# V projected like K and Q, then block-transposed on VectorE, in a fused attention and token-mixing kernel on one core

## The chip, the cores and the metric

The kernel runs on one core of one Trainium2 chip. The metric is the device time of one execution in microseconds, from start to end, as the median of several runs. A core has five engines with a queue each: TensorE (PE in the profile; its weight loads are PEld), VectorE (DVE), ScalarE (ACT), GpSimd (POOL), and SyncE (SP), which here only issues DMA transfers. Each engine works through its own queue strictly in order and meets the others only at semaphores.

## The reference

The program runs two layers, each an attention block followed by a token-mixing block, on x of 2048 tokens and 512 features. Both blocks normalise x and are added to it.

```python
def _A_ref(x, wqkv, wo):
    B, S, D = x.shape
    H = 32; Dh = D // H; W = 256
    qkv = (x @ wqkv).reshape(B, S, 3, H, Dh).transpose(2, 0, 3, 1, 4)
    q, k, v = qkv[0], qkv[1], qkv[2]
    scores = jnp.einsum("bhqd,bhkd->bhqk", q, k) * (Dh ** -0.5)
    idx = jnp.arange(S)
    mask = (idx[:, None] - idx[None, :] >= 0) & (idx[:, None] - idx[None, :] < W)
    p = _softmax(jnp.where(mask, scores, -1e9), axis=-1)
    o = jnp.einsum("bhqk,bhkd->bhqd", p, v)
    return o.transpose(0, 2, 1, 3).reshape(B, S, D) @ wo

def _B_ref(x, w1, b1, w2, b2):          # _layernorm(x) first
    u = _gelu(jnp.einsum("bsd,sf->bdf", h, w1) + b1)
    return (jnp.einsum("bdf,fs->bds", u, w2) + b2).transpose(0, 2, 1)

for _ in range(2):
    x = x + _A_ref(_layernorm(x), A_wqkv, A_wo)
    x = x + _B_ref(_layernorm(x), B_w1, B_b1, B_w2, B_b2)
```

There are 32 heads of only 16 features, and each query sees its own key and the 255 before it. V is the last third of `x @ wqkv`.

## The kernel before

**Tiling.** The tokens are taken in four quarters Q of 512, the heads in four head tiles t of eight heads (128 features). Within a quarter and head tile, attention runs over blocks of 32 queries and 32 keys, and the 9 key blocks that a query block can see are handled in 9 steps m. A step is a score product (`emit_scores`, L631), an exponential on ScalarE over up to 128x1024 (`emit_exp`, L642), a product with the 0/1 edge of the window on VectorE or POOL (L659), and the weighted sum with V (`emit_pv`, L680). Score and sum use TensorE as four 64x64 tiles. There are 288 steps in all.

**K, Q and V.** `project` (L477 to 485) makes K and Q for one head tile and one quarter: four products of 128x128 weights with 512 tokens, accumulated in one PSUM bank. `masked` (L487 to 499) writes the result twice into `k_sb` or `q_sb`, each copy with the other half of the rows zeroed, on VectorE in one instruction or on ScalarE in two. V is made otherwise: `job_v` (L535 to 553) takes 128 tokens and all heads, and for every 32 tokens it uses the normalised tokens as 128x32 weights at four column positions of the array, so that 32 tokens of a key block land on 32 partitions for each of four groups of heads: 64 matmuls of 128 columns. `masked` then writes V into `v_sb`, again twice with the other group zeroed. Next to each V block stands a block of ones (`put_ones`), which makes the sum also deliver the softmax denominators.

**V's place.** `v_all` holds a ring of five slots n of 8 key blocks; the inner order is key block, then group of heads. A quarter's V takes two neighbouring slots, and quarter 2's wraps around. A weighted sum waits for everything in `v_held(Q)` (L607): the V of all heads of the quarter and of the eight blocks before it. Two slots of the ring also serve as scratch in the token-mixing block (`u_part`, L807).

**The token-mixing block.** The first product uses w1 in `w1buf` and in freed attention buffers (L802), part of it (`job_u_part`) already during attention, then Gelu; the second product (`job_y`, L871) adds into x. In the first layer most of the second product is worked into the attention of the second.

**What sets the order.** The code creates its operations in the order of due times and numbers them. The engine and the place of each in that engine's queue are then read from the written-out table `ORDER` (two characters an operation). Banks 6 and 7 are shared by all K, Q, V, output and normalising products (`misc_bank`), in a written-out order `BANKS`; banks 0 to 3 hold scores, 4 and 5 the weighted sums. `Plan.emit` gives every operation the semaphore waits of what it reads and overwrites; a wait on its own engine's earlier reading is left out. Seven buffers `p_sb` hold the exponentials between step and sum.

**Around the sums.** After the ninth step the sums leave banks 4 and 5 (`copy_out`, L328 on VectorE, L330 on ScalarE), their denominators go through small DMAs to a reciprocal (`job_inverse`) and are spread by a small product (`job_normalise`, L724, multiplied at L731); `job_outproj` (L598, L602) closes the block. x is normalised at L418 to L449.

Of the kernel before, what the change touches and what calls it, by code (L numbers as in the profile page):

```python
# [6 lines left out]
dt = mybir.dt  # L7
# [3 lines left out]
P = 128  # L11
# [18 lines left out]
AkAlAmAnAoBFApAqBDArBHAsBJBNBLDOBPBRBlBnCKBpBjCUDgBtCjCPCaCwAtCeC+CICTCpDwF0C2CdCiCoCvC1C6DCEIEaDJDQCtEqC5DbDADGDWE9FaDjDNDVDoGGDtDzDaDiDnD4GQEDDsDyEL  # L30
D3D8ERHjEWEKEdGeEiEQEnEVEcEtEhEyG7E5EmEsExFAE2FVFcE-FhFmFUFZFsFgFwFlF3GtGBGJFrFvF2F6GNHuGTGIGMGaGSGgHIGlGpGZGwI1GdHBGkG3GoGvG0HLHFG9HAHaHEHSHKHRHmJ+Hf
HZH3HeHlHqHrHwIDIPH7H6H+IGIMIHIaIXILISIRJsIyItKlI6IWIcIxI+KyJGI3JKLmJSI9JFJWJJJRJVJjLbJnJiJmJvJuJyJ5KIKBKAKFKEKLHOKSKKKRKYKWKdKhJBH-KoKVKuLGKcKgKnK4Kr
K9JNLDLALKLSK3K8MRHVLXLCLJLeK0LRLjLWLdLvLiLoL3LzL7LNNAL-MDMwLyMJL2L+MCMOOdMUMIMNMdN3MnMTMtNeM3MaMkM9MgMGNFMsNJO2M2NWM8NENaMYNjNINVNuNZOONyNgN5NhMbN9Nn
OEPoOKNxN2N8ODOROJOVOHOaOQOUOiOZOfOpMiOvOzOsO9OoOuPCOlOyO8PIPBPQMqPXPhPHO4PlPPPWPaPrPUPvPkPqP0PuPzP-PLQFQnQJQTQPP+QaQEQIQOQeQXP4QkQsM0M6QxQ2QdQjQrQwQ1
RERDP8QhRHRIRJR+R7SBSHR8SKSESFRTR-R9RWSCSIRlRdSGRhRZSDSLR1R2SAR3SVSNSTSdSeSJSRShR4SpStSuSiSlSmSXR5SqSxSyR6SMSPSZSbTOS+TDTETPS-TJTKTyTzTrTnT3TjT4ThTsXV
TlXWTpTcUEUGTdTwVhViUSUKUOUIUWUbWyUQWzUpUaUkUhVnUuU1UjUoUyU+UtU6VRWmVFU0VMU5V3VTU9VEVYVJWDVdVqY7WEVvV0VQVXVcWVV6VpV-YUVuWQVzV5V+WJWYVCWdWiW7WpXpWXWuW4
WcWhWoWtW+ZNXDXKYCW3W9XCXHXRXkZBXrXwXOXQX1XjXoX6XvX0X5X+X9YFZwYPYXZCYEYIYbZxYhYoYeYuYWYaYgYzYna1Y3YrY+YsZaZTZJYyaVaWY2ZXZdZPY9ZGZkaFZsZSZWZcZjZ2ZrZ1Z9
Z6cDaCaOa4aSa5Z8afaBZgaHajanaqataRaaaiayabbFamasbKbNbSaxbWbZa3bebJbPbicVbqbVbubdbhbpb7blb-btb6b+cFcGcJcQZncYdKcdcXcjcgcqcccicwd+c1cpctc5dzdAc0c4c-dGdD
dQc9dUdaeedidPdTdZdqdhdMdpdvd2eqf4d7eHcudueLeTd1ddeXd6eAebe5eheKeOenfJeteWeaege2dlfAemfGgReseze9fQfWfZePfefFfPfVfifdfhfvdXfzfufyf9hTgIf6gMexf7gTgXgBg3
gegkgLgogQgrgWgvgde0g0gjgqg8gugzg5hDe7hJhNhGhXhChIg-hchMhihWiChqghhxhbh7hQhhhphwh-h0iFiSiJh+iEiOipiZiIiNifhlijiYieitjBi0iii4ioixfDi+jGfNhujLi3i9jFjQjK  # L40
jPjdjeiWkVjhjijjfTkWkhi7kXkYkejwkfkZjtkkkij-j7kgjzj3kbkcklkPkQkakdkRk3kvkxkjkrknlHk4lIk7ktk8k-lDlAlLlMkSkmkTlEkUkpk1kzlTlXlYlplUlglllhlclqldlml7lylul3
# [963 lines left out]
```

## Time and profile before

| what | value |
|---|---|
| median of 3 runs | 501.47 us (500.9 to 501.93) |
| profiled execution | 501.36 us |
| its span in the trace | 499.6 us |
| V's matmuls (L546) | 2048, busy 33.6 us, 220 ns each |
| K's and Q's matmuls (L482) | 248, busy 63.2 us, 381 ns each |
| masked V on VectorE (L492) | 25, 1216 ns each |
| masked V on ScalarE (L497) | 7 jobs, 14 instructions, 697 ns each |
| granted TensorE clock | 1.00 throughout, 0.98 in the last 20 us |

The page gives busy time by engine, the span in 40 slices, and the costliest groups of instructions with what ended the idle time before them. Matmuls are pipelined, and their ends are modelled; a row's duration in the timeline therefore overlaps the next row's start, and what a job occupies is the distance from its start to the next one's. Attention of the first layer runs from about 12 to 165 us, its token-mixing block to about 245 us, the second layer's attention to about 405 us, and the rest to the end.

### The profile page before, as it was taken

To read this page: it belongs to the slowest core of one execution; us is meant where nothing else is said; L and a number is where in the kernel's file an instruction comes from. 1 tells how busy PE (TensorE), PEld (TensorE's weight loads), DVE (VectorE), ACT (ScalarE), POOL (GpSimd) and SP (SyncE) were. 2 spreads that over 40 slices of the span, in tenths; PEclk is the share of its full clock that TensorE was granted. 3 is DMA by queue.
4 is the path that set the end of the run, shared out by engine and by line. 5 is a ranking of instruction groups with operands and counts; after the bars stand their busy time and mean duration, and the time that the engine had idled before them with its cause. 6 is when DMAs were issued, how large, how long until landed. Compare 5 with 4: busy or idle time off the path is not lost.

```text
span 499.6 us, 21330 instructions
## 1 busy us (share of the span) xinstructions
PE 484.8 (97%) x9626; PEld 273.6 (55%) x9626; DVE 322.0 (64%) x667; ACT 322.2 (64%) x389; POOL 167.8 (34%) x337
## 2 busy tenths in 40 slices
PE   7899899999999999999999999999999999999997
PEld 6665455665555544444656565666556554444453
DVE  7788777879877560244887577799897666121123
ACT  5888999999999303402678887989999950330000
POOL 4786544427434110001034522643664431000000
PEclk9999999999999999999999999999999999999999
DMA  6433208205008730933020920120221575082533
GB/s 211 82 63 73 55 5 100 38 7 153 26 26 147 221 85 1 253 91 98 14 34 24 184 39 3 48 30 24 70 68 46 156 207 142 1 222 73 157 104 128
DMA packets 82427, 43.85 MB, mean 88 GB/s; under 512 B 18720, under 2 KB 81312, under 8 KB 82336
## 3 DMA queue, kind: packets, MB, share of 16 engines
q1 hardware_dynamic: 78464, 42.48, 33.8%
q0 software_dynamic: 3872, 0.02, 1.4%
q8 instruction: 75, 1.23, 1.0%
q14 instruction: 16, 0.13, 0.1%
HBM read 32.51 MB, written 2.10 MB: 69 GB/s over the span
## 4 chain that ended last, share of the span: by engine, by line
PE 80%; ACT 6%; DVE 6%; issue 3%; POOL 2%; DMA 2%; SPq 0%; POOLq 0%; DVEq 0%; ACTq 0%
PE ps L802 19%; PE ps L871 19%; PE ps L631 11%; PE ps L680 10%; PE ps L482 8%; PE ps L598 6%; ACT p_sb L642 5%; PE ps L546 4%; PE ps L724 2%; POOL p_sb L659 2%; DMA xhT<-xh_sb 1%; DVE o L328 1%; DVE oU L328 1%; DVE oT L731 1%; PE ps L858 1%
## 5 line engine op out<-in xcount | busy, mean ns | idle before, releaser
L642 ACT ACTIVATE p_sb<-ps 128x1024 bf16<-128x1024 f32 (+7 forms) x288 | 261.0, 974 | 26.7 <-PE ps L631 21.1
L659 POOL TENSOR_TENSOR p_sb<-p_sb,edge 128x256 bf16<-128x256 bf16 (+2 forms) x240 | 112.1, 480 | 148.7 <-ACT p_sb L642 132.7
L631 PE MATMUL ps<-q_sb,k_sb 64*64 64x288 bf16 (+8 forms) x2816 | 107.7, 250 | 4.2 <-ACT p_sb L642 3.7
L680 PE MATMUL ps<-p_sb,v_all 64*64 64x288 bf16 (+8 forms) x2816 | 88.4, 246 | 2.0 <-DVE oU L328 1.3
L631 PEld LDWEIGHTS ps<-q_sb,k_sb 64*64 64x64 bf16 x2816 | 52.7, 106 | 51.5 <-ACT p_sb L642 31.4
L680 PEld LDWEIGHTS ps<-p_sb,v_all 64*64 64x64 bf16 x2816 | 59.3, 107 | 13.4 <-issue 6.3
L871 PE MATMUL ps<-uT,w1buf 128*128 128x512 bf16 x280 | 64.4, 379 | 0.0
L482 PE MATMUL ps<-xhT,wqkv 128*128 128x512 bf16 x248 | 63.2, 381 | 0.7 <-DMA xhT<-xh_sb 0.6
L875 DVE SCALAR_TENSOR_TENSOR x_sb<-ps,b2col,x_sb 128x512 bf16<-128x512 f32 x31 | 22.8, 746 | 58.8 <-PE ps L871 58.7
L659 DVE TENSOR_TENSOR p_sb<-p_sb,edge 128x128 bf16<-128x128 bf16 (+2 forms) x160 | 38.2, 256 | 16.2 <-ACT p_sb L642 12.4
L438 POOL TENSOR_TENSOR rstd<-vare,mhalf 128x4 f32<-128x4 f32 x15 | 15.2, 1014 | 95.4 <-DVE vare L436 67.9
L802 PE MATMUL ps<-xh_sb,w1buf 128*128 128x512 bf16 x192 | 46.0, 380 | 0.0
L418 DVE BATCH_NORM_STATS2 stats<-x_sb 128x6 f32<-128x512 bf16 x64 | 42.9, 681 | 3.1 <-DMA x_sb<-in_A_x_dram 2.8
L871 PEld LDWEIGHTS ps<-uT,w1buf 128*128 128x128 bf16 x280 | 26.6, 98 | 32.0 <-issue 1.3
L871 PE MATMUL ps<-uT,oU 128*128 128x512 bf16 x154 | 35.7, 379 | 0.0
L492 DVE TENSOR_TENSOR k_sb<-ps,half 128x1024 bf16<-128x1024 f32 x26 | 31.6, 1219 | 6.2 <-PE ps L482 6.0
L546 PE MATMUL ps<-wqkv,xhT 128*32 128x128 bf16 x2048 | 33.6, 220 | 2.0 <-DVE v_all L492 1.1
L482 PEld LDWEIGHTS ps<-xhT,wqkv 128*128 128x128 bf16 x248 | 19.9, 97 | 26.5 <-issue 4.7
L492 DVE TENSOR_TENSOR q_sb<-ps,even 128x1024 bf16<-128x1024 f32 (+1 forms) x27 | 31.7, 1175 | 2.9 <-PE ps L631 1.5
L546 PEld LDWEIGHTS ps<-wqkv,xhT 128*32 128x32 bf16 x2048 | 29.0, 97 | 7.5 <-issue 2.0
L492 DVE TENSOR_TENSOR v_all<-ps,even 128x1024 bf16<-128x1024 f32 x25 | 30.4, 1216 | 3.0 <-PE ps L546 2.6
L598 PE MATMUL ps<-wo_sb,oT 128*128 128x512 bf16 x128 | 31.9, 381 | 0.0
(81 smaller groups left out, 442.5 us busy)
## 6 DMA issues: line engine op xcount, KB each, us to landing
w1buf<-in_B_w_dram SPq DMA_DIRECT2D x10, 896.0 KB, 6.3
oU<-in_B_w_dram SPq DMA_DIRECT2D x6, 896.0 KB, 7.9
w1buf<-in_B_w_dram SPq DMA_DIRECT2D x10, 512.0 KB
oU<-o SPq DMA_DIRECT2D x16, 256.0 KB, 3.3
k_sb<-in_B_w_dram SPq DMA_DIRECT2D x16, 256.0 KB, 3.2
xhT<-in_B_w_dram SPq DMA_DIRECT2D x8, 256.0 KB, 3.1
q_sb<-in_B_w_dram SPq DMA_DIRECT2D x8, 256.0 KB, 6.1
out_dram<-x_sb SPq DMA_DIRECT2D x15, 128.0 KB, 3.4
```

The costliest lines, as they stand in the source:

```text
L418: dve(lambda e: e.bn_stats(stats[:, t, :], x_sb[:, t, :]), 690, prio, reads=[R("x", t)], writes=[R("stats", t)])
L482: last = e.matmul(ps[:, b, :], lhsT=wqkv[:, c, c0:c0 + P], rhs=xhT[:, buf, c, :], start=(c == 0), stop=(c == 3))
L492: return e.tensor_tensor(dst, src.unsqueeze(2).to_broadcast([P, n, 2, w]), mask[:].unsqueeze(1).unsqueeze(3).to_broadcast([P, n, 2, w]), o ...
L546: last = e.matmul(acc[32 * a:32 * a + 32, k], lhsT=xhT[:, buf, c, t0:t0 + 32], rhs=wv[:, c, :, a, :], start=(k == 0 and c == 0), stop=(k = ...
L598: last = e.matmul(ps[:, b, :], lhsT=oT[:, buf, t, i * P:(i + 1) * P], rhs=wo_sb[:, t, :], start=(t == 0), stop=(t == 3))
L631: last = e.matmul(ps[64 * c:64 * c + 64, 2 * half + r, 32 * i0:32 * i1], lhsT=k_sb[rows, ring, t, kb % 16, :], rhs=q_sb[rows, t, c, 32 * i ...
L642: latest[0] = plan.op({ACT: (170 + int(2 * (512 - c0) * 0.84), lambda e: e.activation(p_sb[:, slot, :, c0:512], ps[:, 2 * half:2 * half + ...
L659: return e.tensor_tensor(v, v, g, op=ALU.mult)
L680: last = e.matmul(ps[64 * r:64 * r + 64, B_O + (c ^ r), 32 * i0:32 * i1], lhsT=v_all[rows, col:col + 64], rhs=p_sb[rows, slot, r, 32 * i0: ...
L802: r = e.matmul(ps[:, b, :], lhsT=blk[:, n, (ft % 2) * P:(ft % 2 + 1) * P], rhs=xh_sb[:, 4 * g + n, :], start=(first and g == quarters[0] a ...
L871: r = e.matmul(ps[:, b, :], lhsT=blk[:, fc, (st % 2) * P:(st % 2 + 1) * P], rhs=uT[:, fc, :], start=(fc == 0), stop=(fc == NFT - 1))
L875: dve(lambda e: e.scalar_tensor_tensor(x_sb[:, st, :], ps[:, b, :], b2col[:, st:st + 1], x_sb[:, st, :], op0=ALU.add, op1=ALU.add), 750, prio,
```

## The change

V is now made by `project`, like K and Q, one job for each quarter and head tile (still 32 jobs): V transposed, features on partitions, 512 tokens in columns. For this the V columns of the weights are loaded into the free third buffer of `w1buf` and re-ordered into `wqkv` by `turn_weights`, four operations of two copies each. The bank is copied to the bf16 buffer `vT`; VectorE transposes it in 32x32 blocks into `vB`, where the tokens of each key block are on 32 partitions; `spread_v` multiplies it by the mask and writes both copies into `v_sb`, on any of three engines (as two operations where the quarter's two slots are not neighbours). `vT` and `vB` exist once. `v_all` is laid out by head tile first, and a weighted sum waits only for its own head tile's V. The V jobs stand later in the order of a quarter. All tables are new; they hold 2541 operations instead of 2457: VectorE 708 instead of 667, ScalarE 376 instead of 365, POOL 365 instead of 333, TensorE 916 and SyncE 176 as before. The tables, `BANKS` among them, are left out below.

```diff
@@ -272,8 +274,11 @@
-        v_all = sb("v_all", [P, 32 + 5 * 8 * 8 * 64])
-        v_sb = v_all[:, 32:].rearrange("p (n k g m) -> p n k g m", n=5, k=8, g=8)
+        VT = 32 + 5 * 16 * 64
+        v_all = sb("v_all", [P, 4 * VT])
+        v_sb = v_all.rearrange("p (t y) -> p t y", t=4)[:, :, 32:VT].rearrange("p t (n x m) -> p t n x m", n=5, x=16)
+        vT = sb("vT", [P, 512])
+        vB = sb("vB", [P, 512])
@@ -339,8 +344,10 @@
-        for c in (1, 0, 2):
+        for c in (1, 0):
             load(wqkv[:, :, c * D:(c + 1) * D], w_src[:, :, c * D:(c + 1) * D], 1 << 19, -100, writes=[R("wqkv", c)])
+        w_nat = w1buf[:, 2, 0:8].rearrange("p s f -> p (s f)").rearrange("p (c f) -> p c f", c=4)
+        load(w_nat, w_src[:, :, 2 * D:3 * D], 1 << 19, -100, writes=[R("w1", 2, 0)])
@@ -384,20 +391,35 @@
-        dve(lambda e: e.tensor_copy(v_all[:, 0:32].rearrange("p (h d) -> p h d", h=2),
-                                    even[:].unsqueeze(2).to_broadcast([P, 2, DH])), 80, -98,
+        dve(lambda e: e.tensor_copy(v_all.rearrange("p (t y) -> p t y", t=4)[:, :, 0:32].rearrange("p t (h d) -> p t h d", h=2),
+                                    even[:].unsqueeze(1).unsqueeze(3).to_broadcast([P, 4, 2, DH])), 80, -98,
             reads=[R("even")], writes=[R("ones", -1, 0)])
-        def put_ones(n, i, prio, after=(), engines=(DVE, POOL, ACT), writes=()):
-            d = v_sb[:, n, 4 * i:4 * i + 4].rearrange("p k g (s h d) -> p (k g) s h d", h=2, s=2)[:, :, 1, :, :]
-            m = even[:].unsqueeze(1).unsqueeze(3).to_broadcast([P, 32, 2, DH])
-            on = {DVE: (1150, lambda e: e.tensor_copy(d, m)), POOL: (1030, lambda e: e.tensor_copy(d, m)),
-                  ACT: (1000, lambda e: e.activation(d, m, ACTF.Copy))}
-            plan.op({e: on[e] for e in engines}, reads=[R("even")] + list(after), writes=[R("ones", n, i)] + list(writes), prio=prio)
-        for n in range(2):
-            for i in range(2):
-                put_ones(n, i, -97, engines=(ACT,))
+        def put_ones(t, n0, n1, prio, after=(), engines=(DVE, POOL, ACT), writes=()):
+            k = 16 * (n1 - n0)
+            d = v_sb[:, t, n0:n1].rearrange("p n x (s h d) -> p (n x) s h d", h=2, s=2)[:, :, 1, :, :]
+            m = even[:].unsqueeze(1).unsqueeze(3).to_broadcast([P, k, 2, DH])
+            on = {DVE: (36 * k, lambda e: e.tensor_copy(d, m)), POOL: (32 * k, lambda e: e.tensor_copy(d, m)),
+                  ACT: (31 * k, lambda e: e.activation(d, m, ACTF.Copy))}
+            plan.op({e: on[e] for e in engines}, reads=[R("even")] + list(after), writes=[R("ones", n, t) for n in range(n0, n1)] + list(writes), prio=prio)
+        for t in range(4):
+            put_ones(t, 0, 2, -97, engines=(ACT,))
+        def turn_weights(c):
+            d = wqkv[:, c, 2 * D:3 * D].rearrange("p (t a r d) -> p t r a d", t=4, a=4, r=2)
+            o = w_nat[:, c].rearrange("p (t r a d) -> p t r a d", t=4, r=2, a=4)
+            def f(copy):
+                def g(e):
+                    for r in range(2):
+                        last = copy(e)(d[:, :, r], o[:, :, r])
+                    return last
+                return g
+            plan.op({DVE: (500, f(lambda e: e.tensor_copy)), POOL: (1000, f(lambda e: e.tensor_copy)),
+                     ACT: (900, f(lambda e: lambda a, b: e.activation(a, b, ACTF.Copy)))},
+                    reads=[R("w1", 2, 0)], writes=[R("wqkv", 2, c)], prio=-96)
+        for c in range(4):
+            turn_weights(c)
@@ -481,7 +503,8 @@
-            pe(f, 866, prio, reads=[R("wqkv", which)] + [R("xhT", buf, i) for i in range(4)], writes=[BK(b)])
+            pe(f, 866, prio, reads=([R("wqkv", 2, c) for c in range(4)] if which == 2 else [R("wqkv", which)]) + [R("xhT", buf, i) for i in range(4)],
+               writes=[BK(b)])
@@ -532,25 +555,40 @@
-        def job_v(Q, i, prio):
-            b, buf = misc_bank(), Q % 2
-            acc = ps[:, b, :].rearrange("p (k n) -> p k n", k=4)
-            wv = wqkv[:, :, 2 * D:3 * D].rearrange("p c (g a d) -> p c g a d", a=4, d=DH)
-            def f(e):
-                for k in range(4):
-                    for c in range(4):
-                        for a in range(4):
-                            t0 = i * P + 32 * k
-                            last = e.matmul(acc[32 * a:32 * a + 32, k], lhsT=xhT[:, buf, c, t0:t0 + 32], rhs=wv[:, c, :, a, :],
-                                            start=(k == 0 and c == 0), stop=(k == 3 and c == 3), skip_group_check=True,
-                                            tile_position=(0, 32 * a))
+        def spread_v(t, n0, n1, o, held, prio):
+            k = 16 * (n1 - n0)
+            d = v_sb[:, t, n0:n1].rearrange("p n x (s h d) -> p (n x) s h d", h=2, s=2)[:, :, 0, :, :]
+            src = o.rearrange("p (k d) -> p k d", d=DH)
+            def both(e):
+                return e.tensor_tensor(d, src.unsqueeze(2).to_broadcast([P, k, 2, DH]),
+                                       v_all[:, 0:32].rearrange("p (h d) -> p h d", h=2).unsqueeze(1).to_broadcast([P, k, 2, DH]), op=ALU.mult)
+            def each(e):
+                for h in range(2):
+                    last = e.tensor_scalar(d[:, :, h], src, even[:, h:h + 1], None, op0=ALU.mult)
                 return last
-            pe(f, 900, prio, reads=[R("wqkv", 2), R("xhT", buf, i)], writes=[BK(b)], mode="columns", area=866)
-            n, k0 = v_slot(Q, 4 * i)
-            dst = v_sb[:, n, k0:k0 + 4].rearrange("p k g (s h d) -> p (k g) s h d", h=2, s=2)[:, :, 0]
-            masked(b, prio, dst, ps[:, b, :].rearrange("p (r d) -> p r d", d=DH), even, "even", [R("v", n, k0 // 4, h) for h in range(2)])
+            def act(e):
+                for h in range(2):
+                    last = e.activation(d[:, :, h], src, ACTF.Copy, scale=even[:, h:h + 1])
+                return last
+            plan.op({DVE: (150 + 17 * k, both), POOL: (52 * k, each), ACT: (450 + 27 * k, act)}, reads=[R("vB"), R("ones", -1, 0), R("even")],
+                    writes=held, prio=prio)
+        def job_v(Q, t, prio):
+            b = project(Q, 2, 2 * D + t * P, prio)
+            copy_out(vT[:], ps[:, b, :], b, prio, 680, [R("vT")])
+            plan.ops[-1].deps = dict.fromkeys(plan.ops[-1].deps, 0)
+            turn = dve(lambda e: e.transpose(vB[:], vT[:]), 640, prio, reads=[R("vT")], writes=[R("vB")])
+            turn.deps = dict.fromkeys(turn.deps, 0)
+            n0, n1 = v_slot(Q, 0)[0], v_slot(Q, 8)[0]
+            if n1 == n0 + 1:
+                spread_v(t, n0, n0 + 2, vB[:], [R("v", n, t) for n in (n0, n1)], prio)
+            else:
+                for i, n in enumerate((n0, n1)):
+                    spread_v(t, n, n + 1, vB[:, 256 * i:256 * i + 256], [R("v", n, t)], prio)
@@ -565,7 +603,7 @@
-            order = ["k1", "q1", "v0", "v1", "k2", "q2", "v2", "o0", "k3", "q3", "o1", "v3", "K0", "Q0", "o2", "o3"]
+            order = ["k1", "q1", "k2", "q2", "k3", "q3", "v0", "o0", "v1", "v2", "o1", "v3", "K0", "Q0", "o2", "o3"]
@@ -604,14 +642,12 @@
-        def v_held(Q):
-            first = 16 * Q - (8 if Q > 0 else 0)
+        def v_held(Q, t):
             held = [R("ones", -1, 0)]
-            for g in range(first, 16 * Q + 16, 4):
-                n, k = v_slot(0, g)
-                held += [R("v", n, k // 4, 0), R("v", n, k // 4, 1), R("ones", n, k // 4)]
+            for g in range(16 * Q - (8 if Q > 0 else 0), 16 * Q + 16, 8):
+                n, _ = v_slot(0, g)
+                held += [R("v", n, t), R("ones", n, t)] + ([R("ones", n - 1, t)] if n > 0 else [])
@@ -676,7 +712,7 @@
-                            col = 64 * (64 * vn + 8 * vk + 2 * t + r) + (0 if c else 32)
+                            col = VT * t + 64 * (16 * vn + 2 * vk + r) + (0 if c else 32)
@@ -684,7 +720,7 @@
-               reads=[R("p", slot)] + v_held(Q), writes=[BK(B_O), BK(B_O + 1)])
+               reads=[R("p", slot)] + v_held(Q, t), writes=[BK(B_O), BK(B_O + 1)])
@@ -806,9 +842,8 @@
-            n, i = 3 + ft // 4, ft % 4
-            flat = v_sb[:, n].rearrange("p k g m -> p (k g m)")
-            return flat[:, 1024 * i:1024 * i + 1024].bitcast(dt.float32), [R("v", n, i // 2, 0), R("v", n, i // 2, 1), R("ones", n, i // 2)]
+            n, t = 3 + ft // 4, ft % 4
+            return v_sb[:, t, n].rearrange("p x m -> p (x m)").bitcast(dt.float32), [R("v", n, t), R("ones", n, t)]
@@ -906,8 +941,8 @@
-                for i in range(2):
-                    put_ones(n, i, p + 5 * n, [R("xh", 3)], (POOL,))
+                for t in range(4):
+                    put_ones(t, n, n + 1, p + 5 * n, [R("xh", 3)], (POOL,))
@@ -957,9 +992,8 @@
-                for n in (3, 4):
-                    for i in range(2):
-                        todo.append((base + 126, lambda p, n=n, i=i: put_ones(n, i, p, engines=(POOL,), writes=[R("v", n, i, h) for h in range(2)])))
+                for ft in range(NPART):
+                    todo.append((base + 126, lambda p, n=3 + ft // 4, t=ft % 4: put_ones(t, n, n + 1, p, engines=(POOL,), writes=[R("v", n, t)])))
```

## The prediction

> **What bounds the kernel now.** I read the page's first two parts first, then the busy time by stretches, the waits, the PE timeline and the groups by shape. The first line to read is the busy time of the engines.
>
> ```profile
> span 499.6 us, 21330 instructions
> PE 484.8 (97%) x9626; PEld 273.6 (55%) x9626; DVE 322.0 (64%) x667; ACT 322.2 (64%) x389; POOL 167.8 (34%) x337
> ```
>
> TensorE is busy for 484.8 of 499.6 us, so the span is TensorE's work plus 14.8 us of gaps. The busy time by stretches (columns: us, then PE, PEld, DVE, ACT, POOL busy, clock, DMA) shows where they lie.
>
> ```profile
> 12.00:30.00 18.00, 16.06 (x549) 10.84 (x548) 13.60 (x31) 15.59 (x27) 11.64 (x25) 1.00 0.50 92
> 30.00:50.00 20.00, 18.97 (x572) 11.82 (x570) 17.85 (x33) 18.16 (x26) 16.02 (x43) 1.00 0.28 54
> 50.00:70.00 20.00, 17.36 (x537) 10.47 (x538) 15.24 (x34) 19.43 (x24) 10.65 (x24) 1.00 0.16 37
> 70.00:90.00 20.00, 19.43 (x544) 11.68 (x546) 15.52 (x24) 19.18 (x21) 10.22 (x19) 1.00 0.51 64
> 110.00:130.00 20.00, 20.00 (x490) 11.44 (x479) 19.13 (x44) 18.65 (x22) 11.62 (x20) 1.00 0.34 97
> ```
>
> From 12 to 90 us TensorE idles 1.9 + 1.0 + 2.6 + 0.6 = 6.1 us while ScalarE, which computes the exponentials, has 19.4 of 20 us at the worst place. Here ScalarE sets the pace. Elsewhere TensorE does: at 110 to 130 it is full, and the second layer (285 to 385) loses 2.0 us. The rest of the 14.8 lies at both ends, which the change does not aim at. The waits name the same pair:
>
> ```profile
> PEld ps L631 <- ACT p_sb L642: 31.4, 81, 0.7
> PE ps L631 <- ACT p_sb L642: 3.7, 13, 0.5
> ```
>
> **TensorE's price of V.** In the PE timeline the start of the next row, not the modelled end, tells what a job occupies (columns: start, us, operation, count).
>
> ```profile
> 31.70 0.56 PE L631 MATMUL ps<-q_sb,k_sb 64*64 64x288 bf16 x16
> 32.22 1.98 PE L546 MATMUL ps<-wqkv,xhT 128*32 128x128 bf16 x128
> 34.13 0.33 PE L680 MATMUL ps<-p_sb,v_all 64*64 64x288 bf16 x8
> ...
> 46.86 0.41 PE L631 MATMUL ps<-q_sb,k_sb 64*64 64x288 bf16 x8
> 47.10 0.34 PE L680 MATMUL ps<-p_sb,v_all 64*64 64x288 bf16 x8
> 47.34 0.40 PE L631 MATMUL ps<-q_sb,k_sb 64*64 64x288 bf16 x8
> 47.67 1.04 PE L482 MATMUL ps<-xhT,wqkv 128*128 128x512 bf16 x4
> 48.64 0.39 PE L631 MATMUL ps<-q_sb,k_sb 64*64 64x288 bf16 x8
> ...
> 73.61 1.08 PE L546 MATMUL ps<-wqkv,xhT 128*32 128x128 bf16 x64
> 74.62 0.41 PE L631 MATMUL ps<-q_sb,k_sb 64*64 64x96 bf16 x12
> ```
>
> One V job alone occupies 74.62 - 73.61 = 1.01 us, two in a row 34.13 - 32.22 = 1.91: the second costs 0.90. One K job alone occupies 48.64 - 47.67 = 0.97; two in a row (29.87 to 31.70 in the same timeline) 1.83: the second costs 0.86. V becomes such a K job, so 32 jobs x (0.90 - 0.86) = **1.3 us less**. That is all that the 2048 small matmuls give back, because they already ran side by side: 64 of 0.22 us each fit into 1.01 us.
>
> Leaving the 64x64 form for another has a price of its own. The first job of a pair costs 0.11 more than the second, and a group of scores ahead of a job lasts 0.33 (47.34 to 47.67) where one ahead of other 64x64 work lasts 0.24: about 0.1 at each change of form. Numbering the operations as the code creates them, I read the old and new order of TensorE: 259 changes of form before (seven of them between V's form and the full one), 272 after. 13 x 0.1 = **1.3 us more**, all of it in the first layer (114 to 127). TensorE's own work therefore stays as it was, and gaps decide.
>
> **The other engines,** counted from the new tables (32 V jobs; 24 full-size and 16 half-size placements, since one quarter's V wraps around the ring of five):
> - VectorE: 25 masked placements go (25 x 1.216 = 30.4). It takes 25 copies of 0.685 (row of the f32 copies) = 17.1, 32 transposes, 14 full and 7 half placements. A two-input operation of this kind took 0.248 at 128 elements and 0.308 at 256, 0.47 ns an element; carried to 1024 and 512 that is 0.67 and 0.43, so 12.4. No transpose is in the trace. Below stands the 128x512 bf16 copy from PSUM, 0.42, above the 128x1024 placement, 1.22; I take 0.66, nearest to the 0.685 for 512 elements: 21.1, with ends of 13 and 39. Operations that the table moves off VectorE (9 output copies, 9 normalisations, against 4 more Q masks and a few edges) give 5.5 back. Sum: **+15 us**, ends +7 and +33.
> - ScalarE: 7 masked V (1.39 each, two instructions) go, 9.7; 7 copies of 0.60, one full and one half placement, and moved work, among it 9 output copies, come to 9.5. **Unchanged.**
> - POOL: 9 full and 8 half placements at two passes each; a pass over 128x512 took 0.816 there, so 14.7 + about 7, and 7 more normalisations, 5.7: with the rest **+30 us** on 167.8.
>
> On VectorE half of the 15 us falls in the first layer, 125 us of work in 12 to 165 becoming 132 of 153. It is hidden while a mask is no later than the score that needs it; the thin place is 110 to 130, which has 0.87 us free.
>
> The start: V's weights land in a corner of the first-product buffer and are re-ordered by ScalarE (one of four), VectorE (one) and POOL (two), some 0.5 to 1 us each by the 0.35 and 0.49 of the nearest 128x128 and 128x256 rows, in two passes. ScalarE has before its first exponential one re-ordering, one half Q and one normalisation instead of one V: 0.9 + 0.95 + 0.81 - 1.4 = 1.3 us later. By the first score of the fourth head tile of quarter 0 it is 0.6 us ahead again (17.7 against 18.3 us of work that is not exponentials). Their load keeps its place in SP's queue, so the weights land as early as before. I take nothing for the start, between 0 and +1.3.
>
> **Where a gain can come from.** In the old table all four V jobs of quarter 0 had to be done before any weighted sum; now the sum of a head tile waits for its own V job. The new order starts the first sum after 16.3 instead of 18.5 us of TensorE work. Above all it moves filler: up to the first score of quarter 2 (about 86 us here) TensorE now does 80.4 us of work instead of 76.5 (both with jobs at the durations above), while ScalarE's other work up to there is 18.3 us in both. ScalarE sets that point, so 3.9 us of what was idle can be work, and there were 6.1 of idle. At the end of the first layer's scores the lead is still 1.8, plus the 1.3 of changes of form that lie in it. Ends: 3.9 us if ScalarE's pace holds; nothing if later masks and edges open new gaps; and a loss, below. I take half of the upper end, **2.0 us**, near the 1.8 that is left at the end of the layer. The second layer has the same TensorE work up to each quarter (318.3 us before quarter 2 in both), so I count nothing there.
>
> Sum against the profiled execution of 501.36 (its span of 499.6 and 1.76 around it): -1.3 + 1.3 - 2.0 = 499.4. The median of the runs, 501.47, lies 0.1 above that execution, so I say **499.5 us**.
>
> **The rivals.**
> 1. The work only moves: what is gained before 86 us is idle later, as ScalarE and TensorE end the layer together anyway. Only the TensorE terms remain, between -0.9 and +0.5: about 501.4. For it: ScalarE keeps 18.7 of 20 us in 130 to 150. Against it: TensorE is at 20.00 in 110 to 130, so early filler spares time there.
> 2. Slower, by VectorE's queue. The buffers between copy, transpose and placement are single. The transpose waits for the copy and for the previous placement, on POOL in 17 of 40 cases and behind POOL's edges; queued behind that transpose are the masks of K and Q, the output copies and the edges, for which TensorE waits in banks 6 and 7 and in the sums. The trace has such cases: 1.1 us for a V mask, 1.3 for output copies. If each of the 32 transposes holds VectorE 0.3 us longer than the plan and half of it reaches TensorE, that is 4.8 us; without the gain, 501.4 + 4.8 = **506**, and with the gain, 504. It decides once the chain's lateness passed on exceeds 2.0 / 32 = 0.06 us a job. For it: VectorE at 19.13 of 20. Against: most V jobs are ordered many us before their use.
> 3. Contention of VectorE and POOL. The trace has one shape in two settings: the normalisation on 128x512 took VectorE 0.403 in the quiet start and 0.504 under POOL's load. Both get more two-input or two-pass work. If each of 17 POOL placements delays an edge by half a pass, 0.4 us, and 40% of that reaches TensorE, 2.7 us: 499.5 + 2.7 = 502.2. [...]
> 4. The jobs do not come out as K jobs, say because re-ordered weights are late: 1.1 us of stall once, 500.6. Small; kept inside the range.
>
> [...]
>
> **How the numbers follow.** Forecast 499.5 with chance 0.45 (own range 497.5 to 500.4); rival 1 0.18; rival 2 0.25; rival 3 0.07; rival 4 0.05. The range runs from the full 3.9 us with V's 1.3 unspoilt (501.47 - 5.2 = 496.3, rounded up to 496.5, as not all of it can come) to 504, rival 2 with the gain kept; beyond it I leave about 0.1 on the upper side. A measurement here can tell about 0.2%, 1 us, from no change: faster means below 500.47, slower above 502.47. Faster 0.51 (forecast, rival 4 and a little of 1), same 0.20, slower 0.29 (rival 2 and part of 3).
>
> **What would show it.** V's rows as four 128x512 matmuls with 0.97 alone; PE idle in 12 to 90 down from 6.1 to about 4; ScalarE's busy time within 2 us of 322; VectorE near 337 and POOL near 198; transposes near 0.66. It is wrong if TensorE's waits name V's copy, a K or Q mask or an output copy for more than a microsecond in sum beyond now, or if transposes are above 0.9 us.

## The result, and the profile after

The changed kernel takes **506.36 us** (median of 4 runs, 506.14 to 507.63) beside 501.7 for the kernel before on the same chip: a ratio of 1.0097, interval 1.0073 to 1.0122. It is slower by about 4.7 us, outside the forecast range. Its profiled execution took 506.47 us, with a span of 504.7. First the page's busy time by engine.

```profile
span 504.7 us, 17619 instructions
PE 484.0 (96%) x7706; PEld 255.6 (51%) x7706; DVE 341.8 (68%) x709; ACT 323.8 (64%) x392; POOL 217.1 (43%) x388
```

TensorE's work is what it was (484.0 against 484.8), so the span grew by gaps: 20.7 us instead of 14.8. VectorE rose by 19.8 where 15 were expected, ScalarE by 1.6, POOL by 49.3 where 30 were expected. The same stretches as in the prediction:

```profile
12.00:30.00 18.00, 16.07 (x206) 7.59 (x204) 16.16 (x36) 15.85 (x26) 17.01 (x35) 1.00 0.47 75
30.00:50.00 20.00, 18.47 (x321) 8.96 (x321) 19.75 (x39) 17.51 (x26) 17.46 (x39) 1.00 0.27 56
50.00:70.00 20.00, 16.40 (x468) 9.65 (x464) 17.82 (x41) 17.57 (x20) 15.66 (x33) 1.00 0.13 44
70.00:90.00 20.00, 19.19 (x428) 10.33 (x424) 17.67 (x41) 17.91 (x21) 14.38 (x21) 1.00 0.47 71
```

TensorE idles 1.9 + 1.5 + 3.6 + 0.8 = 7.9 us from 12 to 90 us; it was 6.1, and about 4 was forecast. ScalarE no longer sets the pace: 17.6 us at 50 to 70 instead of 19.4. POOL's column (the fifth busy time) went from 11.64, 16.02 and 10.65 to 17.01, 17.46 and 15.66. What TensorE now waits for is named by the waits, first of its weight loads, then of its products (us in total, times, longest):

```profile
PEld ps L667 <- ACT p_sb L678: 27.8, 70, 0.8
PEld ps L716 <- POOL p_sb L695: 11.6, 20, 1.9
PEld ps L716 <- DVE p_sb L695: 5.4, 9, 1.1
```

```profile
PE ps L716 <- POOL p_sb L695: 4.7, 6, 1.6
PE ps L716 <- DVE p_sb L695: 3.0, 6, 0.9
PE ps L667 <- ACT p_sb L678: 0.8, 2, 0.6
```

The row of the kernel before (there the sum is L680 and the edge L659):

```profile
PEld ps L680 <- POOL p_sb L659: 2.2, 6, 0.4
```

L716 is the weighted sum, L695 the product with the window's edge. Waits of the sums' weight loads for an edge on POOL were 2.2 us before and are 11.6; waits of the sums' products for an edge, none of which is listed before, are 7.7. The wait is for edges, not for V. Why they are late stands in the groups by shape (POOL first, then VectorE), and in POOL's timeline:

```profile
L569 POOL TENSOR_SCALAR v_all<-vB,even 128x512 bf16<-128x512 bf16 x18 | 28.0, 1562 | 2.2 <-DVE vB L584 2.0 <-DVE p_sb L695 0.2
...
L569 POOL TENSOR_SCALAR v_all<-vB,even 128x256 bf16<-128x256 bf16 x16 | 14.8, 936 | 0.3 <-DVE vB L584 0.3
```

```profile
L584 DVE STREAM_TRANSPOSE vB<-vT 128x512 bf16<-128x512 bf16 x32 | 22.5, 704 | 3.8 <-POOL v_all L569 3.1 <-ACT vT L335 0.3
```

```profile
56.55 3.73 POOL L569 TENSOR_SCALAR v_all<-vB,even 128x256 bf16<-128x256 bf16 x4
60.23 0.35 POOL L955 TENSOR_SCALAR_AFFINE_SELECT spread<-spread 128x128 bf16<-128x128 bf16 x1
60.53 0.61 POOL L402 CAST v_all<-even 128x512 bf16<-128x512 f32 x1
61.11 3.10 POOL L695 TENSOR_TENSOR p_sb<-p_sb,edge 128x256 bf16<-128x256 bf16 x6
```

And TensorE's timeline at that place:

```profile
59.84 0.41 PE L667 MATMUL ps<-q_sb,k_sb 64*64 64x224 bf16 x8
61.87 0.42 PE L716 MATMUL ps<-p_sb,v_all 64*64 64x96 bf16 x12 [1.61 <-POOL p_sb L695]
```

The prediction's price of a pass came from this row of the kernel before, the normalisation on POOL:

```profile
L445 POOL TENSOR_SCALAR xh_sb<-x_sb,rstd,shift 128x512 bf16<-128x512 bf16 x20 | 16.2, 816 | 0.8 <-POOL shift L442 0.4
```

A placement pass on POOL (L569) takes 1.562 us, not the 0.816 of the prediction; the 34 passes take 42.8 us instead of some 22. They stand in one queue with the edges: four passes hold it for 3.7 us, the six edges behind start at 61.11, and TensorE loses 1.61 us at one sum.

### The profile page after: what moved, and what is told of

Read it like the earlier page. It is cut to its first block, busy times and chain, and to the rows that moved or that the text cites. A ratio compares the mean times of both kernels' runs of the same rounds, so it can differ in the third digit from the quotient of the medians.

```text
span 504.7 us, 17619 instructions
## 1 busy us (share of the span) xinstructions
PE 484.0 (96%) x7706; PEld 255.6 (51%) x7706; DVE 341.8 (68%) x709; ACT 323.8 (64%) x392; POOL 217.1 (43%) x388
## 3 DMA queue, kind: packets, MB, share of 16 engines
q1 hardware_dynamic: 78464, 42.48, 31.4%
## 4 chain that ended last, share of the span: by engine, by line
PE 65%; DVE 17%; POOL 11%; issue 2%; ACT 2%; DMA 1%; SPq 0%; DVEq 0%; POOLq 0%; ACTq 0%
PE ps L838 18%; PE ps L906 18%; PE ps L504 9%; PE ps L667 8%; PE ps L716 7%; POOL v_all L569 6%; POOL p_sb L695 3%; PE ps L636 3%; ACT p_sb L678 2%; DVE stats L440 2%; DVE p_sb L695 2%; DVE q_sb L515 2%; DVE k_sb L515 2%; PE ps L760 1%; DVE vB L584 1%
## 5 line engine op out<-in xcount | busy, mean ns | idle before, releaser
L678 ACT ACTIVATE p_sb<-ps 128x1024 bf16<-128x1024 f32 (+8 forms) x288 | 263.0, 972 | 34.5 <-PE ps L667 28.5
L695 POOL TENSOR_TENSOR p_sb<-p_sb,edge 128x64 bf16<-128x64 bf16 (+2 forms) x234 | 109.0, 481 | 109.0 <-ACT p_sb L678 89.8
L504 PE MATMUL ps<-xhT,wqkv 128*128 128x512 bf16 x376 | 95.9, 382 | 4.1 <-issue 1.5
L716 PE MATMUL ps<-p_sb,v_all 64*64 64x288 bf16 (+8 forms) x2816 | 90.3, 247 | 8.0 <-POOL p_sb L695 4.7
L716 PEld LDWEIGHTS ps<-p_sb,v_all 64*64 64x64 bf16 x2816 | 58.4, 107 | 27.9 <-POOL p_sb L695 11.6
L695 DVE TENSOR_TENSOR p_sb<-p_sb,edge 128x256 bf16<-128x256 bf16 (+2 forms) x166 | 44.5, 282 | 11.6 <-POOL p_sb L695 7.2
L504 PEld LDWEIGHTS ps<-xhT,wqkv 128*128 128x128 bf16 x376 | 30.3, 97 | 43.5 <-issue 7.7
L569 POOL TENSOR_SCALAR v_all<-vB,even 128x512 bf16<-128x512 bf16 (+1 forms) x34 | 42.8, 1268 | 2.5 <-DVE vB L584 2.3
L515 DVE TENSOR_TENSOR q_sb<-ps,even 128x1024 bf16<-128x1024 f32 (+1 forms) x30 | 35.8, 1195 | 4.9 <-PE ps L504 4.8
L838 PE MATMUL ps<-xh_sb,k_sb 128*128 128x512 bf16 x128 | 31.4, 380 | 0.0
L878 DVE TENSOR_TENSOR v_all<-v_all,ps 128x512 f32<-128x512 f32 x12 | 8.1, 687 | 33.1 <-PE ps L838 33.1
```

What stands on the lines that cost most here:

```text
L504: last = e.matmul(ps[:, b, :], lhsT=wqkv[:, c, c0:c0 + P], rhs=xhT[:, buf, c, :], start=(c == 0), stop=(c == 3))
L515: return e.tensor_tensor(dst, src.unsqueeze(2).to_broadcast([P, n, 2, w]), mask[:].unsqueeze(1).unsqueeze(3).to_broadcast([P, n, 2, w]), o ...
L569: last = e.tensor_scalar(d[:, :, h], src, even[:, h:h + 1], None, op0=ALU.mult)
L678: latest[0] = plan.op({ACT: (170 + int(2 * (512 - c0) * 0.84), lambda e: e.activation(p_sb[:, slot, :, c0:512], ps[:, 2 * half:2 * half + ...
L695: return e.tensor_tensor(v, v, g, op=ALU.mult)
L716: last = e.matmul(ps[64 * r:64 * r + 64, B_O + (c ^ r), 32 * i0:32 * i1], lhsT=v_all[rows, col:col + 64], rhs=p_sb[rows, slot, r, 32 * i0: ...
```

## The experiments

There are three theories. **A, POOL's queue:** the placement passes are dear and hold up the edges behind them. **B, VectorE's queue** (rival 2 of the prediction): the chain of copy, transpose and placement holds up VectorE, and what waits behind the transposes is late. **C:** the new order itself loses. The kernel before took 501.84 us beside experiments 1, 2, 3 and 7, 502.44 beside 5, 6 and 8, and 501.71 beside 4 and 9; each ratio is to the value beside it. These three differ by 0.7 us, and so uncertain are differences in us between experiments of different groups.

**1. Cheaper passes on POOL.**

```diff
-            plan.op({DVE: (150 + 17 * k, both), POOL: (52 * k, each), ACT: (450 + 27 * k, act)}, reads=[R("vB"), R("ones", -1, 0), R("even")],
+            def plain(e):
+                for h in range(2):
+                    last = e.tensor_copy(d[:, :, h], src)
+                return last
+            plan.op({DVE: (150 + 17 * k, both), POOL: (52 * k, plain), ACT: (450 + 27 * k, act)}, reads=[R("vB"), R("ones", -1, 0), R("even")],
```

> The changed kernel, but POOL's 17 placements of V write each copy by a plain copy without the mask (the mask of these placements is left out); order, counts and all other engines stay. In the changed kernel POOL's 34 masked passes took 42.8 us (1.56 us for 128x512, 0.94 for 128x256); a copy pass in the same pattern took 0.61 us for 128x512 there (the ones), so about 17 us are expected. Theory A (POOL's placement passes are dear and make the window edges behind them late, for which TensorE's sums wait): the time falls to 501 to 502.5 us, and the idle time of the sums that is put down to edges falls from 24.7 us on PE and PEld to under 10. Theory B (VectorE's longer queue, with transposes and single buffers, holds TensorE): 505.5 to 507, as VectorE has the same work. Theory C (the new order itself loses): 505.5 to 507.

495.11 us, ratio 0.9864 (0.9839 to 0.9888). The copies took 612 and 410 ns, POOL 191.3 us instead of 217.1, and the sums' weight loads waited 4.3 us for POOL's edges instead of 11.6. With nothing else changed, 26 us off POOL's queue give 11.3 us: the whole loss and a gain besides. A's expectation had the direction right and was far too small (501 to 502.5). C is out, for the order is the same.

**2. POOL's placements moved behind their transposes on VectorE.** Only two lists of `ORDER` differ: 17 entries leave POOL's and stand in VectorE's (the first, `By`, is shown).

```diff
-...BqBtBwBuFgBxCzB4Fk...
+...BqBtBwBuFgBxByCzB4Fk...
...
-...EC9ByDEC3DFCO...
+...EC9DEC3DFCO...
```

> The changed kernel, but POOL's 17 placements stand in VectorE's queue, each right behind its transpose, in VectorE's one-instruction form (0.77 us full, 0.43 half): POOL has 43 us less, VectorE about 10 us more (342 to 352). Theory A: 501 to 503.5 us. Theory B: 508 to 510, because VectorE's queue is longer still. Theory C: about 506.

501.58 us, ratio 0.9995 (0.9979 to 1.0011). POOL fell to 178.5 us and VectorE rose to 348.3. The time is 4.8 us below the changed kernel, but 6.5 above experiment 1: VectorE's queue is no free place either.

**3. POOL's load alone, on the kernel before.** The same 34 passes, at the like places of POOL's queue, into a scrap buffer that nothing waits for.

```diff
+                e.tensor_scalar(junk[:, k0:k0 + k, h], junk_in[:].unsqueeze(1).to_broadcast([P, k, DH]), even[:, h:h + 1], None, op0=ALU.mult)
```

> The kernel before, with 34 extra passes on POOL of the same kind and sizes (masked writes of 512 or 256 elements into a scrap buffer that nobody reads), each pair behind the edge that comes nearest in the order to where the changed kernel places V on POOL. Nothing else is changed; VectorE, ScalarE, TensorE and the order are those of before. Theory A: POOL rises from 168 to about 205 or 210 us and the time by 2 to 5 us, to 503.5 to 506.5. Theories B and C: within 0.7 us of before, since POOL had 330 us free and nobody waits for the extra writes.

523.64 us, ratio 1.0424 (1.0387 to 1.0460): right in sign, but 21.8 us where 4.7 was the upper end of what was expected. The passes took 42.6 us as in the changed kernel. The waits of the sums' weight loads, then two windows:

```profile
PEld ps L692 <- POOL p_sb L671: 16.0, 11, 3.1
PE ps L692 <- POOL p_sb L671: 12.1, 7, 2.9
```

```profile
50.80:54.20 3.40, 1.13 (x44) 0.84 (x40) 1.81 (x6) 1.63 (x3) 2.97 (x8) 1.00 0.51 124
54.20:61.00 6.80, 5.42 (x87) 3.44 (x88) 3.54 (x11) 5.43 (x8) 4.31 (x11) 0.50 0.00 0
```

Single waits reach 3.1 us, and the clock column shows a second cost: TensorE is busy for 1.13 of 3.4 us, and the granted clock is 0.50 for the next 6.8 us. Three more stretches of 3.4 us at 0.50 begin at 84.9, 136.1 and 313.6 us, with TensorE busy for 1.52, 0.75 and 0.67 us of the 3.4 us ahead of each. These are 17.0 us in all; if half of them is lost, 8.5 of the 21.8 us are the clock's, an estimate and an upper end. What sets the lower clock off is not shown; that it is the scarce work ahead of it is the author's reading of these four places, where the sums' products waited for at most 2.9 us at a time. In the changed kernel's profiled execution the clock stays at 1.00, so this is no part of its loss; by that reading it shows how fast the price of a late edge grows.

**4. The same load with a cheaper form** (see 6):

```diff
-                e.tensor_scalar(junk[:, k0:k0 + k, h], junk_in[:].unsqueeze(1).to_broadcast([P, k, DH]), even[:, h:h + 1], None, op0=ALU.mult)
+                e.tensor_scalar(junk[:, k0:k0 + k, h], junk_in[:].unsqueeze(1).to_broadcast([P, k, DH]), even[:, h:h + 1], zero[:, 0:1], op0=ALU.mult, op1=ALU.add)
```

> The kernel before with the same 34 extra POOL passes at the same places as in the run that rose to 523.6 us, but in the two-operation form, 0.79 and 0.58 us instead of 1.56 and 0.92: 23 us instead of 43. If the loss goes with the load, 22 x 23 / 43 = 12 us: 513. If it is single long blocks of 3.1 us that make a sum late and set off a fall of the granted clock, much less: 503 to 507, with a granted clock above 0.995.

507.08 us, ratio 1.0105 (1.0086 to 1.0124), clock 0.999. With passes of 768 and 571 ns, 22.7 us in all, the loss is 5.4 us: 53% of the load, a quarter of the loss. The price is not proportional to POOL's busy time. Much of that is the clock by the estimate above: without its 8.5 us, experiment 3 loses 13.3 us for 42.6, or 0.31 us for each us, beside 0.24 here. That long single blocks cost more than their share in another way as well is not shown. What is shown is that even passes at about the assumed price are not free on POOL.

**5. What makes a pass dear.** Forms over 128x256, each run twice, on an idle POOL late in the kernel before.

> The kernel before, with seven forms of a POOL pass over 128x256 run twice at the end of POOL's queue, one after the other, when POOL has nothing else to do. Theory A1: one-operation masked pass 0.92 us both in strips of 16 and on contiguous rows; two-operation pass 0.45 in both; plain copy 0.41 in strips. Theory A2: contiguous rows 0.45 in all forms, strips 0.92 in both masked forms. The last form multiplies by a constant instead of a per-partition operand: 0.45 if the operand is what costs, 0.92 if it is the single operation. The time stays that of before.

The instructions by tile, with their shortest, median and longest ns:

```profile
L988 POOL TENSOR_SCALAR form_out<-form_in,even x2: 917/948/979, 427.1 to 432.3; 128x256 bf16<-128x256 bf16 x2
L989 POOL TENSOR_SCALAR form_out<-form_in,even,form_zero x2: 555/556/556, 428.1 to 433.3; 128x256 bf16<-128x256 bf16 x2
L990 POOL TENSOR_SCALAR form_out<-form_in,even x2: 917/918/918, 428.8 to 434.0; 128x256 bf16<-128x256 bf16 x2
L991 POOL TENSOR_SCALAR form_out<-form_in,even,form_zero x2: 554/555/556, 429.8 to 435.0; 128x256 bf16<-128x256 bf16 x2
L992 POOL COPY form_out<-form_in x2: 393/394/396, 430.4 to 435.6; 128x256 bf16<-128x256 bf16 x2
L993 POOL COPY form_out<-form_in x2: 400/400/400, 430.9 to 436.1; 128x256 bf16<-128x256 bf16 x2
L994 POOL TENSOR_SCALAR form_out<-form_in x2: 847/848/849, 431.4 to 436.6; 128x256 bf16<-128x256 bf16 x2
```

```diff
+            lambda e: e.tensor_scalar(to[:, :, 0], s3, even[:, 0:1], None, op0=ALU.mult),
+            lambda e: e.tensor_scalar(to[:, :, 1], s3, even[:, 0:1], zero[:, 0:1], op0=ALU.mult, op1=ALU.add),
...
```

L988, L989 and L992 write strips of 16 as the placement does, L990, L991 and L993 write contiguously. The pattern makes hardly any difference; the form does. A multiplication alone takes 0.92 us, a multiplication and an addition 0.555 (0.45 was expected). L994 multiplies by a constant: 0.848, so the single operation costs, and the per-partition operand little. This is one execution; the full kernels show like prices (936 ns in the changed one, 579 in the next experiment).

**6. The changed kernel with two-operation passes.** A zero is added to each product, which leaves the values as they are; `mhalf0` holds the zeros.

```diff
+                    last = e.tensor_scalar(d[:, :, h], src, even[:, h:h + 1], mhalf0[:, 0:1], op0=ALU.mult, op1=ALU.add)
-            plan.op({DVE: (150 + 17 * k, both), POOL: (52 * k, each), ACT: (450 + 27 * k, act)}, reads=[R("vB"), R("ones", -1, 0), R("even")],
+            plan.op({DVE: (150 + 17 * k, both), POOL: (52 * k, pair), ACT: (450 + 27 * k, act)}, reads=[R("vB"), R("ones", -1, 0), R("even")],
```

> The changed kernel, but each masked pass on POOL multiplies by the mask and adds a zero from a per-partition operand, the form of the normalisation that took 0.81 us for 128x512 there; the result is the same. Theory A1 (the slow thing is the one-operation form of the pass, 1.56 us where the prediction put 0.82): passes of 0.8 to 0.9 and 0.4 to 0.5 us, 22 us in all instead of 43, and by the line between plain copies (17 us of passes, 495.1) and the changed kernel (43 us, 506.4) a time of 496.5 to 499. Theory A2 (the slow thing is the pattern, 16 elements out of every 64): passes stay at 1.5 and the time at 506. Theory B (VectorE's queue): 506, whatever the passes take; it is already spoken against by the plain copies.

**496.73 us, ratio 0.9882 (0.9857 to 0.9906)**: faster than both kernels, 9.6 us below the changed one. Its page and its passes by shape:

```profile
span 494.8 us, 17520 instructions
PE 469.4 (95%) x7606; PEld 256.0 (52%) x7706; DVE 339.4 (69%) x709; ACT 323.3 (65%) x392; POOL 197.1 (40%) x389
```

```profile
L579 POOL TENSOR_SCALAR v_all<-vB,even,zero 128x512 bf16<-128x512 bf16 x18 | 14.0, 786 | 2.2 <-DVE vB L594 1.4 <-DVE rc L754 0.6 <-DVE p_sb L705 0.2
...
L579 POOL TENSOR_SCALAR v_all<-vB,even,zero 128x256 bf16<-128x256 bf16 x16 | 9.1, 579 | 0.3 <-DVE vB L594 0.3
```

23.1 us of passes and POOL at 197.1 us: what the prediction had put, 22 and 198. (100 records of products are missing here, 7606 beside 7706 weight loads, so PE's busy time says nothing.)

**7. One two-input instruction on POOL in place of two passes.**

```diff
-            plan.op({DVE: (150 + 17 * k, both), POOL: (52 * k, each), ACT: (450 + 27 * k, act)}, reads=[R("vB"), R("ones", -1, 0), R("even")],
+            plan.op({DVE: (150 + 17 * k, both), POOL: (52 * k, both), ACT: (450 + 27 * k, act)}, reads=[R("vB"), R("ones", -1, 0), R("even")],
```

> The changed kernel, but POOL places V by one two-input multiplication instead of two masked passes. By the slope of POOL's edges (0.31, 0.43 and 0.67 us at 64, 128 and 256 elements: 1.9 ns an element) a full placement is 2.1 us instead of 3.1 and a half one 1.15 instead of 1.87: 28 us instead of 43. Theory A: about half of the loss comes back, 503 to 504.7 us. Theories B and C: 505.5 to 507.

503.23 us, ratio 1.0030 (1.0011 to 1.0048), inside A's range, but by luck: at experiment 1's price the 13.8 us less on POOL would give about 500. The instructions took 28.5 us (2133 and 1164 ns), only 5 us more than the passes of experiment 6, but the kernel took 6.5 us more. The sums' weight loads waited 8.9 us for edges on VectorE, where experiment 6 has 2.4. One such place in the timelines of VectorE, POOL and TensorE:

```profile
74.48 3.52 DVE L695 TENSOR_TENSOR p_sb<-p_sb,edge 128x128 bf16<-128x128 bf16 x1
```

```profile
74.62 1.16 POOL L564 TENSOR_TENSOR v_all<-vB,v_all 128x512 bf16<-128x512 bf16 x1
75.75 0.42 POOL L695 TENSOR_TENSOR p_sb<-p_sb,edge 128x128 bf16<-128x128 bf16 x1
76.13 1.15 POOL L564 TENSOR_TENSOR v_all<-vB,v_all 128x512 bf16<-128x512 bf16 x1
77.25 0.66 POOL L695 TENSOR_TENSOR p_sb<-p_sb,edge 128x256 bf16<-128x256 bf16 x1
```

```profile
78.05 0.41 PE L716 MATMUL ps<-p_sb,v_all 64*64 64x256 bf16 x8 [2.52 <-DVE p_sb L695]
```

A VectorE edge of 0.31 on average lasts 3.52 us, about as long as POOL has four two-input instructions in a row (74.62 to 77.91), and TensorE waits 2.52 us for it. Right behind it, from 78.3 us, the granted clock is 0.50 for 3.4 us. This is read as rival 3's contention, from the times alone; what holds the edge up is not shown. In the changed kernel it stays small: there the longest edge on VectorE took 0.81 us (0.74 before), and two took 0.28 us together at 47.82, in the middle of two one-input POOL passes (46.89 to 50.01).

**8. More work for VectorE.** Each V job transposes 160 columns more, into a scrap buffer: 338 ns, 10.8 us in all.

```diff
+                e.transpose(vC[:], vT[:, 0:160])
+                return e.transpose(vB[:], vT[:])
```

> The changed kernel, with five of the sixteen blocks of every transpose done once more into a scrap buffer ahead of the transpose: VectorE gets 32 x about 0.35 us = 11 us more, in the same queue places; nothing else changes. Theory A (POOL's passes set the new stalls): 506 to 508, at most 0.15 us of time for each us of VectorE. Theory B (VectorE's queue holds TensorE): 508.5 to 512, 0.2 to 0.5 us for each us. For scale: the loss against before is 4.7 us for 20 us more of VectorE and 49 more of POOL.

510.14 us, ratio 1.0160 (1.0124 to 1.0197): 3.8 us over the changed kernel (3.2 by the two ratios), 0.35 us for each us added. That is B's size, and A's part of this expectation fell: VectorE has little room behind the transposes. So both queues are tight. POOL's slope, from experiments 1 and 6, is 11.3 / 25.8 = 0.44 and 9.6 / 20.0 = 0.48 us for each us. These slopes hold near the changed kernel only: in experiment 2 POOL had 38.6 us less and VectorE 9.4 us more of placements, which by the slopes gives about 493, and it took 501.58.

**9. V's cheaper product alone, on the kernel before.** Four products of 512 columns in place of the 64 small ones, each with its 128 tokens four times (V itself is left out).

```diff
-                            last = e.matmul(acc[32 * a:32 * a + 32, k], lhsT=xhT[:, buf, c, t0:t0 + 32], rhs=wv[:, c, :, a, :],
...
+                    last = e.matmul(acc, lhsT=wqkv[:, c, 2 * D + i * P:2 * D + i * P + P],
+                                    rhs=xhT[:, buf, c, i * P:i * P + P].unsqueeze(1).to_broadcast([P, 4, P]),
```

> The kernel before in its own order, with only V's product changed: each V job multiplies 128x128 weights with its 128 tokens repeated four times, four matmuls of 128x512 instead of 64 small ones, and the masked write is as before (V itself is left out of the computation: what is written is not V). The prediction's TensorE term alone: 32 x 0.04 = 1.3 us less, and seven changes of form fewer at 0.1, so 499.6 to 500.6 against 501.7. Rival 1, V's small matmuls are dearer than their starts in the timeline show and are the whole 5.7 us that the version with two-operation passes has against the kernel before: 496 to 498. Rival 2, ScalarE's pace hides it in the first layer: half, 500.8 to 501.4.

502.48 us, ratio 1.0025 (0.9999 to 1.0051): a miss of all three expectations, for there is no gain. The single products are cheaper as worked out (40.83 - 39.87 = 0.96 us between starts, where the kernel before has 1.01), yet the lead does not last. TensorE's timeline, this kernel and then the kernel before:

```profile
42.24 0.36 PE L628 MATMUL ps<-q_sb,k_sb 64*64 64x288 bf16 x8 [0.30 <-ACT p_sb L639]
...
44.90 1.04 PE L543 MATMUL ps<-xhT,wqkv 128*128 128x512 bf16 x4 [0.69 <-DMA xhT<-xh_sb]
```

```profile
42.41 0.36 PE L631 MATMUL ps<-q_sb,k_sb 64*64 64x288 bf16 x8 [0.30 <-ACT p_sb L642]
...
44.78 1.08 PE L546 MATMUL ps<-wqkv,xhT 128*32 128x128 bf16 x64 [0.40 <-DMA xhT<-xh_sb]
```

A lead of 0.17 us at 42 us is gone at 44.8, where the V job waits for its transfer. The wait of the scores' weight loads for exponentials is 38.3 us here and was 31.4. In the old order, then, the saved time turned into waiting, at least at this place.

## Why the prediction was wrong

**The step that failed** is the term for POOL: "a pass over 128x512 took 0.816 there, so 14.7 + about 7". That row was the normalisation, which multiplies and adds. The added pass only multiplies, and was taken to be no dearer; it took 1.562, and the term 42.8. Nothing of before shows the one-operation form, and while the transpose, unseen as well, was bounded from both sides, this operation was not. With passes of about the assumed price (experiment 6) the kernel takes 496.7 us, at the lower end of the forecast range; the term's error of 20 us on POOL is worth the 9.6 us between 496.73 and 506.36 (10.8 by the two ratios).

**The second failure** is that POOL's 30 us were summed and then given no place. The forecast's sum has no term for it. The prediction asked of VectorE what is queued behind; of POOL it asked this only in rival 3, where each of 17 placements delays an edge by 0.4 us, half a pass, and 2.7 us come of it, with a chance of 0.07. The edges wait for whole blocks of up to 3.7 us, by their place in the queue. POOL holds 240 of the edges before and 234 after, and TensorE waits for them. At about the assumed price such passes cost 5.4 us on the kernel before (experiment 4), so the price of a pass is not the whole of the error.

**Rival 2** gave the time (506) and the kind of loss, a queue behind V's placement that makes edges late, but the wrong engine as its source: VectorE's transposes waited for POOL's placements only twice, 3.1 us in all. That its time was met is luck: it leaves out a gain of 5.7 us that is there, and prices another queue. Its warning about VectorE was right as a slope (0.35, where it assumed a half). Its chance of 0.25 was too low, and its upper end of 504 with the gain kept ended the range too soon.

**The expected gain** came, and was larger than forecast, 5.7 us instead of 2.0, and not where it was expected. Rival 1, that the work only moves, falls with it. The starts of some exponentials in the three traces (us from the span's start):

| exponential | before | changed | two-operation passes |
|---|---|---|---|
| first of layer 1 | 15.7 | 16.2 | 16.0 |
| last of layer 1 (144th) | 163.7 | 168.9 | 163.7 |
| first of layer 2 | 244.6 | 243.1 | 237.9 |
| last of layer 2 | 401.8 | 407.6 | 398.0 |
| end of the span | 499.6 | 504.7 | 494.8 |

Between the second and the third column POOL's slow passes cost 5.2 us up to the end of layer 1's scores and 4.4 us in layer 2's (164.5 against 160.1); between the layers they cost nothing. Against the kernel before, the good version (experiment 6) is level at the end of layer 1's scores, and 6.7 us ahead by the first exponential of layer 2 (74.2 us between the two instead of 80.9); layer 2's scores then take 160.1 instead of 157.2.

TensorE's busy time tells where the work went (in the changed kernel, whose trace has every product and whose order is the good version's). Up to the last exponential of layer 1 it is 155.8 us instead of 153.9: 1.9 us of work done early, as the prediction's 1.8 had it. Between the layers TensorE is full in both, for 74.2 and 80.9 us. So up to layer 2's first exponential it does 230.0 us instead of 234.8, and by the last one both have done 390: 4.8 us of work have moved into the attention of layer 2, whose scores take 2.9 us more in the good version. "I count nothing there", of the second layer, therefore failed. No experiment took this order apart, so it is argued, and the gain as a whole (5.7 us) is what is shown.

**The other terms.** V's job as four products of 128x512 is right: L504 has 376, 248 for K and Q and 128 for V, at 382 ns; but the 1.3 us saved there gave nothing when put alone (experiment 9). Transposes 0.704 against 0.66. VectorE's full placement 0.769 against 0.67, the half one 0.57 against 0.43; with the transposes these are 3.7 of the 4.8 us by which VectorE's sum was short. ScalarE within 2 us, right. The test of idle time, 6.1 down to about 4, failed at 7.9. The start costs 0.5 us up to the first exponential, inside its 0 to 1.3. The other signs of being wrong did not point at the cause: TensorE's products waited 1.2 us in all for V's copy, the masks and the output copies instead of 2.6, its weight loads 7.5 instead of 4.8, and no sign named the edges.

**Open:** why the cheaper product alone gives nothing over the whole span, and how the gain of the new order divides between the order and V by head tile. The new V under the old order was not tried, since a job now needs all 512 tokens of its quarter.

## What to carry to other kernels

Take a price from a row with the same engine, shape and number of operations in the instruction; one operation fewer need not be cheaper (on POOL, over 128x256, 0.92 us with one and 0.555 with two). When work goes to an engine with a low busy share, look for what stands behind it in that queue and who waits for that, and look at the longest single block as well as the sum: with blocks of 3.1 us the granted clock fell too (experiment 3, mean 0.984), with blocks of 1.5 us it did not (experiment 4, 0.999); in the changed kernel, with blocks of up to 3.7 us, it stayed at 1.00.

## What was not expected of the hardware

On POOL, TENSOR_SCALAR with one operation took 0.92 us over 128x256, in strips or contiguous, and 1.56 over 128x512 in strips; with a second operation that changes nothing, 0.555 over 128x256, in strips or contiguous, and 0.79 over 128x512 in strips. A plain copy took 0.39 over 128x256. In experiment 7 a two-input edge on VectorE, 0.31 us on average, lasted 3.52 us (74.48 to 78.00) while POOL ran four two-input operations back to back (74.62 to 77.91); in the changed kernel two edges took 0.28 us together beside one-input passes on POOL (46.89 to 50.01), the one place shown. And in experiment 3 the granted TensorE clock fell to 0.50, once for 6.8 and three times for 3.4 us; in the 3.4 us ahead of each fall TensorE was busy for 0.67 to 1.52 us. In the changed kernel, where TensorE's longest gap was 1.61 us, it did not fall.
